# Attention, short convolution and gated projection on one core: transposes by halves of rows, a new order of the pieces, and GpSimd steps tied to VectorE

## The chip, the core and the metric

The kernel runs on one core of a Trainium2 chip. The metric is the device time of one execution in microseconds (us), the median of three runs. A core has TensorE (PE in the profile; its weight loads are PEld), VectorE (DVE), ScalarE (ACT), GpSimd (POOL) and SyncE (SP), which here issues all the DMAs.

## The reference

```python
scores = scale * np.matmul(q_c, k_c.transpose(0, 1, 2, 4, 3))     # chunks of 64 rows, 8 heads, 8 batches
scores = scores - np.max(scores, axis=-1, keepdims=True)
attn = np.exp(scores)
attn = attn / (np.sum(attn, axis=-1, keepdims=True) + 1e-09)
out = np.matmul(attn, v_c)                                        # x: (8, 576, 512)
...
for k in range(5):
    gate_pre += conv_w[k][None, None, :] * xp[:, k:k + S, :]      # causal convolution of x over the sequence
gate = 1.0 / (1.0 + np.exp(-gate_pre))
val = x @ w_val
return (gate * val @ w_out).astype(np.float32)
```

Everything is float32; q, k and v are (8, 8, 576, 64), the two weights (512, 512).

## The kernel before, in words

The tokens are cut into nine groups of 512 (g = 0 to 8; group 8 holds the last 64 of each batch), and each group into two halves of the channels (p = 0, 1). Such a (g, p) is called a pair here: 18 pairs, each with 32 blocks of 64 by 64 scores.

The program is a list of some 1,030 pieces, written out by hand in the string ORDER (line 19), and each engine runs its pieces in that order. A piece is a name and its indices. For a pair: `S` scores (64x64 matmuls in the four quarters of the array; the trace shows two instructions for each one of the program), `mx` row maxima, `sb` and `ex` (or `ng` and `ea`) subtraction and exponential, `sm` (or `rc`) row sums and reciprocals, `nm` normalising, `T` transposing the probabilities on TensorE (eight 128x128 transposes into a bank of PSUM), `ec` copying them out, `A` probabilities times v (64x64 matmuls again), `xr`, `xd` and `xc` the rounded value, its remainder and a plain copy of x. Then `V` the product with w_val, `vc` its copy, `k0` and `k` (`kx`, `kk` for two groups at once) the taps of the convolution, `sg` the sigmoid, `gs` gate times value, `gr` and `gd` its rounded value and remainder, `P` the product with w_out, `oc` and `st` copy and store. Each float32 product is made of three 128x128 by 128x512 matmuls: high by high, low by high, high by low, so V and P each need both parts of x and of the gated value. `w1` to `w9`, `wa`, `wb` and `Q` split the weights in the same way at the start. A `D` behind a name puts the piece on VectorE, a `G` (only in the changed kernel) on GpSimd.

Pair (0, 1) is done in two halves at the start, so that the first products can begin early. What sets the order around the change is this list alone, with two more tables: SLOTS, which says which buffer and which of the four double banks of PSUM a tile gets (a tile waits until the one before it in its slot has been read), and the pieces' own data. SyncE's DMAs are issued in the list's order too, eight in flight.

Lines that matter here: `tr` (369), `ec` (380), `av` (388), the loop over the list (602 to 609). Every operation goes through `run` in line 139, so the profile shows line 139 for all of them and they are told apart by their tiles.

Of the kernel before, what the change touches and what calls it, by code (L numbers as in the profile page):

```python
# [18 lines left out]
ORDER = """zw,lw v 1,zr 1,zr 0,lc,zi,zs 0,zs 1,lw v 3,lw v 2,w1 v 1,w5 c 0,w1 c 0,w2 v 1,w3 v 1,w5 v 1,w4 v 1,w2 c 0,w3 c 0,w5 v 3,  # L19
w7 v 1,w1 v 3,w6 v 1,w8D v 1,w2 v 3,w4 c 0,w3 v 3,W 9 22,Q v 1,lk 0 1 0,lq 0 1 0,w1 v 2,w4 v 3,w2 v 2,w3 v 2,w5 v 2,w6D v 3,  # L20
S 0 1 0,lk 0 0 0,lk 0 1 1,lq 0 1 1,lq 0 0 0,lk 0 0 1,lq 0 0 1,w4 v 2,wc v 1,mx 0 1 0,w6 v 2,w7 c 0,ng 0 1 0,w7 v 2,ea 0 1 0,ra 0 1 0,
W 3,S 0 1 1,w8D v 2,S 0 0 0,mx 0 1 1,w8D c 0,w9,ng 0 1 1,w7 v 3,S 0 0 1,lw v 0,lk 1 0,lq 1 0,lv 0 1,lw o 3,ea 0 1 1,ra 0 1 1,
rr 0 1 0,Q v 2,w8 v 3,mx 0 0,nm 0 1 0,sb 0 0,Q v 3,w5 v 0,w1 v 0,ex 0 0,T 0 1 0,w3 v 0,rr 0 1 1,S 1 0 0,wc v 2,sm 0 0,
nm 0 1 1,S 1 0 1,ec 0 1 0,w2 v 0,A 0 1 0,lk 1 1,lq 1 1,lv 0 0,lv 1 0,wc v 3,mx 1 0,T 0 1 1,nm 0 0,xr 0 1 0,ec 0 1 1,
V 0 2 2 0,sb 1 0,V 0 3 2 1,w5 o 3,A 0 1 1,xc 0 1 0,xr 0 1 1,w4 v 0,T 0 0,xc 0 1 1,xd 0 1 0,V 0 2 3 0,w6D v 0,V 0 3 3 0,
ec 0 0,V 0 2 3 1,w1 o 3,S 1 1 0,w7 v 0,ex 1 0,xd 0 1 1,A 0 0,w8 v 0,k0 0 2,sm 1 0,S 1 1 1,wa v 0,xc 0 0,V 0 0 2 0,V 0 2 2 1,
V 0 0 3 1,V 0 0 2 1,xr 0 0,mx 1 1,V 0 1 2 0,nm 1 0,V 0 0 3 2,V 0 3 3 1,k0 0 0,V 0 3 2 2,V 0 2 3 2,xd 0 0,V 0 3 1 0,
V 0 1 2 1,V 0 0 0 0,V 0 3 3 2,V 0 3 0 0,lw o 0,lw o 2,lw o 1,w5 o 0,k0 0 3,ng 1 1,k 0 0 1,T 1 0,k0 0 1,wbD v 0,V 0 0 0 2,
w2 o 3,V 0 3 2 0,k 0 0 2,V 0 2 1 1,ec 1 0,V 0 2 0 0,V 0 0 1 0,k 0 3 1,V 0 1 0 0,V 0 2 0 1,ea 1 1,V 0 2 0 2,w3 o 3,V 0 2 1 2,
k 0 1 1,V 0 3 1 1,V 0 0 2 2,V 0 1 1 1,w4 o 3,V 0 3 0 1,V 0 2 2 2,V 0 3 1 2,w1 o 1,A 1 0,k 0 0 3,w7 o 3,w1 o 0,V 0 1 3 2,  # L30
# [36 lines left out]
V 6 1 2,kk 6 0 3,V 6 0 1,V 6 0 3,k 4 0 4,V 8 1 1,k 4 1 4,V 6 1 0,kk 6 1 2,sg 4 0,V 8 1 3,kx 6 3,gs 4 0,V 6 2 2,V 6 1 3,
k0 8 0,gs 4 1,V 8 1 2,k0 8 1,V 8 0 2,kk 6 2 2,V 8 2 3,vc 8 0,k 3 2 2,V 6 0 2,gr 4 0,kk 6 1 3,V 7 0 0,gr 5 1,V 8 2 2,gdD 4 0,
V 7 1 3,V 6 3 3,kk 6 2 3,V 6 1 1,k 5 1 2,V 8 3 0,k 5 0 2,V 7 1 0,vc 8 1,kk 6 0 4,V 7 1 2,vc 6 0,V 6 2 3,k 3 1 3,gr 4 1,
V 7 0 3,k 5 1 3,P 4 0 0,vc 6 1,k0D 8 2,P 4 0 1,k 5 0 3,gdD 4 1,P 4 2 0,V 7 0 1,k 5 0 4,V 7 0 2,k 5 1 4,P 4 2 1,kk 6 1 4,  # L70
sg 5 0,V 7 2 0,V 7 2 1,kk 6 3 1,sg 6 0,P 4 1 2,k0 8 3,k 3 1 4,P 4 3 1,kk 6 3 2,V 7 2 2,P 4 0 3,gs 5 0,P 4 1 3,V 7 2 3,
gdD 5 1,gr 5 0,V 7 3 0,sg 7 0,kk 6 3 3,P 4 2 3,P 4 0 2,gdD 5 0,V 7 1 1,P 4 1 1,gs 6 0,vc 7 0,P 4 1 0,kk 6 2 4,V 7 3 2,
P 4 3 3,kk 6 3 4,P 4 3 0,P 5 2 0,k 8 1 1,sg 6 1,P 5 2 3,k 3 0 2,oc 4 0,V 7 3 3,k 3 0 3,P 5 2 1,gr 6 0,k 3 2 3,P 5 3 2,
# [21 lines left out]
    b="0 0 1 2 0 2 1 3 2 0 1 3 2 0 1 0 2 0 0 1 3 0 2 3 1 3 3 1 2 3 0 2 1 2 2 3 2 0 1 3 1 2 1 0 1 2 2 3 0 1 0 2 3 1 0 "  # L95
      "1 3 2 3 2 3 0 1 3 2 0 2 3 2 2 3 0 1 2 2 0 1 2 3 0 3 2 1 2 1 3 0 2 1 0 3 2 0 1 3 2 0 1 3 2",
    e="0 1 0 0 0 0 1 1 0 0 0 1 0 1 1 0 1 0",
)

ALONE = 20  # L100
# [566 lines left out]
```

## Time and profile before

| | |
|---|---|
| median of 3 runs | 280.64 us (280.20 to 281.83) |
| profiled execution, first to last instruction | 279.6 us |
| what lies around it, against the median | 1.0 us |
| PE busy | 268.9 us (96%), 3370 matmul instructions |
| DVE busy | 239.5 us (86%) |
| ACT busy | 198.7 us (71%) |
| POOL busy | 59.4 us (21%) |
| moved by DMA | 42.5 MB |
| granted TensorE clock | 1.000 on the mean |

The profile gives the span of one execution; the runs' times also hold what lies before its first and after its last instruction. A busy PE is not a PE at its peak: matmuls are pipelined, and their ends are modelled, so costs on TensorE are read from one start to the next. Times are in us from the span's start.

### The profile page before, as it was taken

The numbers are of one execution on the slowest core, as the hardware profiler recorded it, in microseconds if no ns is written. First come the engines' busy times: TensorE is split into PE (matmuls) and PEld (weight loads), VectorE is DVE, ScalarE is ACT, GpSimd is POOL, SyncE is SP. The second block draws the span as 40 slices with busy tenths as digits, with TensorE's granted clock in tenths as the row PEclk, the third lists the DMA queues.
The fourth block names the chain that finished last, engine by engine and source line by source line (L and its number), as shares of the span: only waits on it lengthen the run. The fifth ranks groups of instructions, "written<-read, shape, count | busy, mean of one in ns | idle before, by whom it ended". The sixth has DMA issues, their size and how long they took to land.

```text
span 279.6 us, 7851 instructions
## 1 busy us (share of the span) xinstructions
PE 268.9 (96%) x3370; PEld 216.6 (77%) x3370; DVE 239.5 (86%) x303; ACT 198.7 (71%) x368; POOL 59.4 (21%) x58
## 2 busy tenths in 40 slices
PE   6598999999998999999999999999999999999995
PEld 3366778887886888888888888888888888888884
DVE  3979999999999988989898998999999998996020
ACT  5899999999997988895958588837644544614402
POOL 1056242049294003061335001100000000300000
PEclk9999999999999999999999999999999999999999
DMA  6999999763831649540082000000000000050656
GB/s 224 395 409 406 406 407 409 290 225 108 281 149 37 192 150 338 189 131 30 2 292 88 2 5 2 0 0 2 0 0 0 4 0 0 16 212 0 241 209 225
DMA packets 14754, 42.46 MB, mean 152 GB/s; under 512 B 1536, under 2 KB 1792, under 8 KB 14720
## 3 DMA queue, kind: packets, MB, share of 16 engines
q1 hardware_dynamic: 14720, 41.97, 40.7%
q8 instruction: 26, 0.43, 0.6%
q14 instruction: 8, 0.07, 0.1%
HBM read 32.53 MB, written 9.44 MB: 150 GB/s over the span
## 4 chain that ended last, share of the span: by engine, by line
PE 89%; DMA 8%; issue 1%; SPq 0%; ACT 0%
PE b L139 89%; DMA z<-in_v 4%; DMA z<-in_moe_w_val 2%; DMA z<-in_q 2%; SPq L139 0%; ACT z L139 0%
## 5 line engine op out<-in xcount | busy, mean ns | idle before, releaser
L139 PE MATMUL b<-z,v_hi 128*128 128x512 f32 x288 | 97.3, 403 | 1.3 <-issue 1.1
L139 PE MATMUL b<-o_hi,z 128*128 128x512 f32 (+1 forms) x296 | 94.5, 391 | 0.0
L139 DVE SCALAR_TENSOR_TENSOR ys<-ys,cw 128x511 f32<-128x511 f32 (+7 forms) x104 | 84.5, 863 | 0.1
L139 ACT COPY z<-b 128x1024 f32<-128x1024 f32 (+2 forms) x53 | 50.3, 970 | 38.3 <-PE b L139 35.5
L139 PEld LDWEIGHTS b<-z,v_hi 128*128 128x128 f32 x288 | 53.8, 188 | 14.5 <-issue 1.7
L139 PEld LDWEIGHTS b<-o_hi,z 128*128 128x128 f32 x296 | 55.1, 188 | 12.6
L139 PE MATMUL b<-o_lo,z 128*128 128x512 f32 (+1 forms) x148 | 57.4, 388 | 0.0
L139 PE MATMUL b<-z,v_lo 128*128 128x512 f32 x144 | 55.9, 394 | 0.0
L139 POOL TENSOR_TENSOR z<-e_row,rs 128x1024 f32<-128x1024 f32 (+1 forms) x15 | 27.0, 1804 | 47.2 <-DVE rs L139 17.0
L139 PEld LDWEIGHTS b<-o_lo,z 128*128 128x128 f32 x148 | 27.8, 188 | 5.9
L139 PEld LDWEIGHTS b<-z,v_lo 128*128 128x128 f32 x144 | 27.1, 188 | 5.4
L139 POOL TENSOR_TENSOR z<-ys,z 128x1024 fp32r<-128x1024 f32 x4 | 10.0, 2527 | 96.9 <-ACT z L139 96.9
L139 ACT ACTIVATE ys<-ys 128x1024 f32<-128x1024 f32 x16 | 16.8, 1059 | 11.0 <-DVE ys L139 10.8
L139 ACT ACTIVATE e_row<-b,mx 128x64 f32<-128x64 f32 x80 | 23.7, 345 | 0.4 <-DVE mx L139 0.4
L139 DVE TENSOR_TENSOR z<-b,z 128x1024 fp32r<-128x1024 f32 (+1 forms) x19 | 22.0, 1161 | 2.3 <-ACT z L139 1.3
L139 ACT CAST z<-ys 128x1024 fp32r<-128x1024 f32 x16 | 16.5, 1048 | 9.0 <-DVE ys L139 9.0
L139 DVE TENSOR_REDUCE mx<-b 128x16 f32<-128x1024 f32 (+1 forms) x19 | 21.6, 1144 | 1.3 <-PE b L139 1.1
L139 PEld LDWEIGHTS b<-z,z 64*64 64x64 f32 x960 | 15.7, 135 | 7.8 <-DMA z<-in_k 2.6
L139 PE MATMUL b<-z,z 64*64 64x64 f32 x960 | 17.6, 221 | 3.7 <-DMA z<-in_q 3.0
L139 ACT CAST z<-b 128x1024 fp32r<-128x1024 f32 (+1 forms) x19 | 18.7, 991 | 2.1 <-PE b L139 2.1
L139 ACT ACTIVATE ys<-ys,cw 128x512 f32<-128x512 f32 (+1 forms) x25 | 19.2, 811 | 0.0
L139 ACT ACTIVATION_READ_ACCUMULATOR e_row<-b,mx 128x1 f32 x80 | 19.0, 238 | 0.0
(74 smaller groups left out, 308.3 us busy)
## 6 DMA issues: line engine op xcount, KB each, us to landing
out<-z SPq DMA_DIRECT2D x16, 512.0 KB, 3.7
z<-in_q SPq DMA_DIRECT2D x10, 512.0 KB, 7.2
z<-in_v SPq DMA_DIRECT2D x9, 512.0 KB, 5.0
ys<-in_v SPq DMA_DIRECT2D x9, 512.0 KB, 10.1
ys<-in_k SPq DMA_DIRECT2D x9, 512.0 KB, 7.3
z<-in_k SPq DMA_DIRECT2D x7, 512.0 KB, 9.4
ys<-in_q SPq DMA_DIRECT2D x6, 512.0 KB, 10.2
z<-in_moe_w_val SPq DMA_DIRECT2D x4, 512.0 KB, 5.4
```

What stands on the lines that cost most here:

```text
L139: return tc.keep_in_program_order(fn(*args, **kwargs))
```

## The change

Three things change.

1. `tr` now transposes a pair in two halves of rows: for each of the eight blocks one transpose of partitions 0 to 63 and one of partitions 64 to 127, with 64 columns each, into the two banks of the tile. The old function stays as `tr_whole` (piece `TW`). In the list, ten pieces are `TW` (the two halves of pair (0, 1) and pairs (0,0), (1,0), (1,1), (2,0), (2,1), (3,0), (3,1), (4,1)), and nine are the new `T`: pairs (4,0) and all of groups 5 to 8. `av` reads the probabilities in either layout.
2. All pieces behind the first 112 come in another order, with other slots. Some go to other engines or another form: two of `ra`/`rr` become `rc`; three `w1` go to GpSimd (`w1G`), two `w2` to VectorE, one `w5` and `w8` become one `w58`; VectorE gets two more `nm`, two more `gd`, four more `k0`, one more `oc` and one more `o1`, and loses one `wa`, one `wb`, one `kx`; pair (8, 1) uses `ng`/`ea`/`rc` in place of `sb`/`ex`/`sm`. In all VectorE has 305 rows in the program's listing in place of 282.
3. A table BEHIND ties 23 pieces on GpSimd to a piece named beside each, all of them of VectorE: the GpSimd step starts only when that one has ended.

```diff
-ORDER = """zw,lw v 1,zr 1,zr 0,lc,zi,zs 0,zs 1,lw v 3,lw v 2,w1 v 1,w5 c 0,w1 c 0,w2 v 1,w3 v 1,w5 v 1,w4 v 1,w2 c 0,w3 c 0,w5 v 3,
+ORDER = """zr 1,zr 0,zw,lw v 1,lc,zi,zs 0,zs 1,lw v 3,lw v 2,w1 v 1,w5 c 0,w1 c 0,w2 v 1,w3 v 1,w5 v 1,w4 v 1,w2 c 0,w3 c 0,w5 v 3,w7 v 1,
...
+BEHIND = {
+    "nm 1 1": "w7 o 3", "w1G o 0": "xd 1 0", "w1G o 1": "mx 2 0", "w8 o 3": "k 1 0 2", "nm 2 0": "sm 2 0",
...
+    "nm 4 1": "sm 4 1", "nm 5 1": "k 2 2 1", "gd 2 1": "gs 2 0", "gd 2 0": "sb 6 0", "nm 5 0": "sm 5 0",
...
-ALONE = 20
+ALONE = 28
...
+    def w58(n, c, b=None):
+        run(V.scalar_tensor_tensor, out=rest(n, c, b)[1], in0=part(raw[n, c][0], b), scalar=2.0**-52,
+            in1=part(wt[n, c], b), op0=ALU.mult, op1=ALU.mult)
...
-    def tr(g, p, b=None):
-        if not b:
+    def tr(g, p):
+        split.add((g, p))
+        et_ps[g, p] = bank()
+        for j in range(8):
+            block = normed[g, p][:, 2 * j:2 * j + 2, :].rearrange("p b k -> p (b k)")
+            for w in range(2):
+                r = slice(w * D, (w + 1) * D)
+                run(E.transpose, out=et_ps[g, p][:, w, j * D:(j + 1) * D], in_=block[r], identity=ident[r, r])
+
+    def tr_whole(g, p, b=None):
+        if (g, p) not in et_ps:
...
-        et = probs_t[g, p].rearrange("p (h b a q) -> p h b a q" if own is None else "p (b h a q) -> p h b a q", h=2, b=2, a=2)
+        if (g, p) in split:
+            et = probs_t[g, p].rearrange("p (w h b a t) -> p h b a w t", w=2, h=2, b=2, a=2)
+        else:
+            et = probs_t[g, p].rearrange("p (h b a w t) -> p h b a w t" if own is None else "p (b h a w t) -> p h b a w t", h=2, b=2, a=2, w=2)
...
+        if piece in BEHIND:
+            sync = mybir.DependencyInfo(mybir.DependencyClass.Sync, mybir.DependencyReason.DATA)
+            tc.add_manual_dep(made[begun].ins, ends[BEHIND[piece]].ins.name, sync, reason="behind")
```

What the list moves is seen in the rows of the engines. First TensorE around the scores of pairs (8, 0) and (7, 1), before: `ident` marks a transpose, 64x64 are scores or probabilities times v, `v_hi` and `v_lo` are the parts of w_val, `o_hi` of w_out.

```order
L139 MATMUL b_2088<-ys 64x64 x32
L139 MATMUL b_2125<-ys,z_1579 64x64 x32
L139 MATMUL b_2162<-ident,z_1944 128x128 x8
L139 MATMUL b_2176<-z_1720,v_hi 128x512
L139 MATMUL b_2176<-z_1720,v_lo 128x512
```

The same place now: the scores of pair (8, 0) are b_2167, and two transposes by halves stand before and between their two parts.

```order
L146 MATMUL b_2106<-ys,z_705 64x64 x32
L146 MATMUL b_2148<-ident,z_2091 128x64 x16
L146 MATMUL b_2167<-z_2101,ys 64x64 x16
L146 MATMUL b_2184<-ident,z_1971 128x64 x16
L146 MATMUL b_2217<-z_1735,v_hi 128x512
L146 MATMUL b_2217<-z_1735,v_lo 128x512
```

Before, one transpose of eight stood behind one unbroken stretch of 64x64 work; now sixteen half transposes stand inside it, and the stretch goes 64x64, halves, 64x64, halves, 128x128.

Next TensorE behind the transpose of pair (0, 0) (the row with `ident`), before: b_459 is probabilities times v of pair (0, 0), b_439 the scores of pair (1, 1), z_390 the rounded x of pair (0, 1).

```order
L139 MATMUL b_419<-ident,z_388 128x128 x8
L139 MATMUL b_393<-z_390,v_hi 128x512 x2
L139 MATMUL b_393<-z_390,v_lo 128x512
L139 MATMUL b_439<-z_373,z_375 64x64 x16
L139 MATMUL b_459<-z_434,z_377 64x64 x32
L139 MATMUL b_515<-z_390,v_hi 128x512
```

The same now: b_456 is probabilities times v of pair (0, 0), b_491 the scores of pair (1, 1), and z_433 the remainder of x of pair (0, 1).

```order
L146 MATMUL b_420<-ident,z_388 128x128 x8
L146 MATMUL b_393<-z_390,v_lo 128x512 x2
L146 MATMUL b_393<-z_390,v_hi 128x512
L146 MATMUL b_448<-z_390,v_lo 128x512
L146 MATMUL b_448<-z_433,v_hi 128x512
L146 MATMUL b_456<-z_435,z_377 64x64 x32
L146 MATMUL b_491<-z_373,z_375 64x64 x32
```

Six products now stand ahead of b_456 where three stood, the last of them reads the remainder z_433, and both parts of the scores of pair (1, 1) have gone behind it.

That remainder is written by VectorE. Its rows up to there, before (z_429 is the remainder, in two halves, z_305 and z_437 are words of the weights, rs_494 the row sums of pair (1, 0)):

```order
L139 TENSOR_TENSOR z_429<-b_356,z_390 128x512
L139 CAST v_hi<-z_305 128x2x256
L139 TENSOR_SCALAR z_437<-z_276 128x512
L139 TENSOR_SCALAR z_305<-z_305 128x512
L139 TENSOR_TENSOR z_429<-b_399,z_390 128x512
L139 TENSOR_REDUCE rs_494<-e_row_65 128x16
```

And now (z_433 is the remainder, z_304 and z_429 the words; the second row on z_429 needs what GpSimd's `w1G` writes):

```order
L146 TENSOR_TENSOR z_433<-b_356,z_390 128x512
L146 TENSOR_SCALAR z_304<-z_304 128x512
L146 CAST v_hi<-z_304 128x2x256
L146 TENSOR_SCALAR z_429<-z_275 128x512
L146 TENSOR_SCALAR z_429<-z_429 128x512
L146 TENSOR_TENSOR z_433<-b_399,z_390 128x512
L146 TENSOR_REDUCE rs_444<-e_row_65 128x16
```

Four short steps stand between the two halves of the remainder where three stood.

## Rows read from the trace of the kernel before

**Rows 1.** The page: busy time, share of the span and instructions of each engine
```profile
PE 268.9 (96%) x3370; PEld 216.6 (77%) x3370; DVE 239.5 (86%) x303; ACT 198.7 (71%) x368; POOL 59.4 (21%) x58
```
**Rows 2.** The chain of waits in order: start, length, what
```profile
13.77 11.88 DMA z<-in_v
...
25.78 5.95 PE b L139 x118
...
84.78 0.90 issue
85.68 191.00 PE b L139 x1883
```
**Rows 3.** Busy time by stretch: PE, PEld, DVE, ACT, POOL; clock, DMA share
```profile
25.80:105.00 79.20, 78.13 (x1224) 63.83 (x1224) 75.15 (x107) 74.71 (x196) 30.13 (x23) 1.00 0.67 246
...
161.00:258.00 97.00, 97.00 (x667) 78.75 (x660) 91.80 (x96) 55.11 (x60) 5.13 (x9) 1.00 0.05 17
```
**Rows 4.** Timeline of PE at two whole transposes: start, length, what
```profile
143.45 1.03 PE L139 MATMUL b<-ident,ys 128*128 128x128 f32 x8
144.32 1.04 PE L139 MATMUL b<-ident,z 128*128 128x128 f32 x8
```
**Rows 5.** Timeline of PE, then of weight loads, around a stretch of 64x64
```profile
74.43 0.63 PE L139 MATMUL b<-z,v_hi 128*128 128x512 f32 x2
74.89 0.40 PE L139 MATMUL b<-z,v_lo 128*128 128x512 f32 x1
75.13 0.39 PE L139 MATMUL b<-z,v_hi 128*128 128x512 f32 x1
75.45 2.10 PE L139 MATMUL b<-z,z 64*64 64x64 f32 x128
77.47 0.50 PE L139 MATMUL b<-o_hi,z 128*128 128x512 f32 x1
77.81 0.39 PE L139 MATMUL b<-o_lo,z 128*128 128x512 f32 x1
...
75.44 1.96 PEld L139 LDWEIGHTS b<-z,z 64*64 64x64 f32 x128 [0.36 <-ACT e_row L139]
```
**Rows 6.** Timeline of weight loads: two of a transpose, two of a product
```profile
22.87 0.14 PEld L139 LDWEIGHTS b<-ident,z 128*128 128x128 f32 x1 [0.43 <-POOL z L139]
22.93 0.14 PEld L139 LDWEIGHTS b<-ident,z 128*128 128x128 f32 x1
...
21.22 0.19 PEld L139 LDWEIGHTS b<-z,v_hi 128*128 128x128 f32 x1 [0.45 <-ACT z L139]
21.33 0.19 PEld L139 LDWEIGHTS b<-z,v_lo 128*128 128x128 f32 x1
```
**Rows 7.** Timeline of DVE, 24 to 28.7 us
```profile
24.20 0.76 DVE L139 TENSOR_SCALAR z<-z 128x512 f32<-128x512 f32 x2
24.88 0.68 DVE L139 TENSOR_TENSOR z<-b,z 128x512 fp32r<-128x512 f32 x1
...
27.49 1.20 DVE L139 TENSOR_REDUCE mx<-b 128x16 f32<-128x1024 f32 x1
```
**Rows 8.** Groups by form: count, busy us, mean ns; a POOL row, then DVE rows
```profile
L139 POOL TENSOR_TENSOR z<-z,z 128x512 f32<-128x512 f32 x5 | 7.4, 1479 | 6.0 <-DVE z L139 6.0
...
L139 DVE TENSOR_TENSOR z<-e_row,rs 128x1024 f32<-128x1024 f32 x3 | 3.6, 1215 | 0.0
...
L139 DVE TENSOR_SCALAR z<-z 128x512 f32<-128x512 f32 x8 | 3.4, 422 | 3.7 <-DMA z<-in_moe_w_val 3.7
```
**Rows 9.** POOL, then PE: normalising and transposing pair (1, 1)
```profile
38.15 1.98 POOL L139 TENSOR_TENSOR z<-e_row,rs 128x1024 f32<-128x1024 f32 x1 [8.44 <-DVE rs L139]
...
41.32 1.03 PE L139 MATMUL b<-ident,z 128*128 128x128 f32 x8
```
**Rows 10.** DVE, then POOL, where the two meet at 242 us
```profile
242.29 4.24 DVE L139 SCALAR_TENSOR_TENSOR z<-tails,cw,z 128x512 f32<-128x512 f32 x3
...
242.40 2.91 POOL L139 TENSOR_TENSOR z<-ys,z 128x1024 fp32r<-128x1024 f32 x1 [66.32 <-ACT z L139]
```
**Rows 11.** DVE's last remainders of the gated value
```profile
255.04 2.36 DVE L139 TENSOR_TENSOR z<-z,z 128x1024 fp32r<-128x1024 f32 x2 [1.11 <-ACT z L139]
```

More of the change, by code (lines that the diff above doesn't have):

```diff
@@ L154, in chunk_attention_gated_conv @@
     (qt, kt, vt, s_ps, probs, normed, et_ps, probs_t, x_ps, xs, xh, xl, acc, v_ps, v_sb, gh, gl, o_ps, o_sb, mxs, rss,
-     raw, wt, wr, wq, w_ps, xs_at, acc_at) = ({} for _ in range(28))
+     raw, pairs, wt, wr, wq, w_ps, w_bank, xs_at, acc_at) = ({} for _ in range(30))
     small = {name: 0 for name in ("mx", "rs")}
     done = {}
+    split = set()
     def count(name):
@@ L169, in piece @@
                 kept[g, p] = z()
+            flat = of[g, p].rearrange(of_flat[len(of.shape)])
             if half is None:
-                run(DMA, out=kept[g, p], in_=of[g, p].rearrange(of_flat[len(of.shape)]))
+                run(DMA, out=kept[g, p], in_=flat)
             else:
-                run(DMA, out=kept[g, p].rearrange("p (b t) -> p b t", b=2)[:, half], in_=of[g, p][:, half])
+                run(DMA, out=twin(kept[g, p])[:, half], in_=twin(flat)[:, half])
         return piece
@@ L177, in chunk_attention_gated_conv, with part, lw, kept_in @@
     lq, lk, lv = load(qt, q), load(kt, k), load(vt, v)
-    def lw(n, c):
-        pair = z(U32)
-        words = pair.rearrange("p (n w) -> p n w", w=2)
-        raw[n, c] = words[..., 0], words[..., 1]
-        run(DMA, out=pair, in_=w_in[n][c * P:(c + 1) * P, :].bitcast(U32))
-    def kept_in(w, n, c):
+    def part(a, b):
+        return a if b is None else a[:, b * 256:(b + 1) * 256]
+    def lw(n, c, b=None):
+        if (n, c) not in pairs:
+            pairs[n, c] = z(U32)
+        both = pairs[n, c].rearrange("p (n w) -> p n w", w=2)
+        raw[n, c] = both[..., 0], both[..., 1]
+        rows = w_in[n][c * P:(c + 1) * P, :].bitcast(U32)
+        if b is None:
+            run(DMA, out=pairs[n, c], in_=rows)
+        else:
+            run(DMA, out=twin(pairs[n, c])[:, b], in_=twin(rows)[:, b])
+    def kept_in(w, n, c, b=None):
         if n == "v":
-            return w[n][:, c // 2 * 2:c // 2 * 2 + 2, c % 2 * 256:(c % 2 + 1) * 256]
+            rows = slice(c // 2 * 2, c // 2 * 2 + 2) if b is None else c // 2 * 2 + b
+            return w[n][:, rows, c % 2 * 256:(c % 2 + 1) * 256]
         return w[n][:, c, :]
-    def unit(a, n):
-        return a.rearrange("p (c m) -> p c m", c=2) if n == "v" else a
+    def unit(a, n, b=None):
+        return a.rearrange("p (c m) -> p c m", c=2) if n == "v" and b is None else a
     def lc():
@@ L219, in w4 @@
-    def w4(n, c):
-        run(V.scalar_tensor_tensor, out=wq[n, c], in0=wt[n, c].bitcast(U32), scalar=3, in1=wq[n, c],
-            op0=ALU.logical_shift_left, op1=ALU.bitwise_or)
-    def w5(n, c):
-        wr[n, c] = pool.tile([P, NH * TAPS], F32, name="cw_r") if n == "c" else z()[:, :T]
-        run(S.mul, wr[n, c].bitcast(F32R) if (n, c) in summed_on_pe else wr[n, c], raw[n, c][0], 2.0**-52)
-    def w6(n, c, copy=S.copy):
-        run(copy, out=kept_in(wh, n, c), in_=unit(wq[n, c].bitcast(F32), n))
@@ L241, in wb @@
-    def wb(n, c, on=G):
-        run(on.tensor_tensor, out=kept_in(wl, n, c), in0=unit(wt[n, c], n), in1=unit(wr[n, c], n), op=ALU.add)
-    def wq_sum(n, c):
-        w_ps[n, c] = unit(bank()[:, 0], n)
-        for i, (lhsT, rhs) in enumerate(((ident, wq[n, c].bitcast(F32)), (signed[:, 1], kept_in(wh, n, c)),
-                                         (signed[:, 0], wr[n, c].bitcast(F32R)))):
-            run(E.matmul, w_ps[n, c], lhsT=lhsT, rhs=rhs if i == 1 else unit(rhs, n), start=i == 0, stop=i == 2)
@@ new lines, in rest, with w5, w6, w7 @@
+    def rest(n, c, b):
+        if (n, c) not in wr:
+            wr[n, c] = z()[:, :T]
+        a = part(wr[n, c], b)
+        return a, a.bitcast(F32R) if (n, c) in summed_on_pe else a
+    def w5(n, c, b=None):
+        run(S.mul, rest(n, c, b)[1], part(raw[n, c][0], b), 2.0**-52)
+    def w6(n, c, b=None, copy=S.copy):
+        run(copy, out=kept_in(wh, n, c, b), in_=unit(part(wq[n, c], b).bitcast(F32), n, b))
+    def w7(n, c, b=None):
+        run(V.tensor_single_scalar, out=part(wt[n, c], b).bitcast(U32), in_=part(wq[n, c], b), scalar=0xFF800000, op=ALU.bitwise_and)
@@ new lines, in wb, with wq_high @@
+    def wb(n, c, b=None, on=G):
+        run(on.tensor_tensor, out=kept_in(wl, n, c, b), in0=unit(part(wt[n, c], b), n, b), in1=unit(part(wr[n, c], b), n, b), op=ALU.add)
+    def wq_high(n, c, b=None):
+        if (n, c) not in w_ps:
+            w_bank[n, c] = bank()
+            w_ps[n, c] = w_bank[n, c][:, 0]
+        ps = unit(part(w_ps[n, c], b), n, b)
+        run(E.matmul, ps, lhsT=ident, rhs=unit(part(wq[n, c], b).bitcast(F32), n, b), start=True, stop=False)
+        run(E.matmul, ps, lhsT=signed[:, 1], rhs=kept_in(wh, n, c, b), start=False, stop=False)
@@ L254, in w9, with wq_low, wq_sum, wc @@
+    def wq_low(n, c, b=None):
+        ps = unit(part(w_ps[n, c], b), n, b)
+        run(E.matmul, ps, lhsT=signed[:, 0], rhs=unit(part(wr[n, c], b).bitcast(F32R), n, b), start=False, stop=True)
+    def wq_sum(n, c, b=None):
+        wq_high(n, c, b)
+        wq_low(n, c, b)
+    def wc(n, c, b=None, copy=S.copy):
+        run(copy, out=kept_in(wl, n, c, b), in_=unit(part(w_ps[n, c], b), n, b))
     def w9():
@@ L262, in sc @@
         own = (g, p) in HALVES
-        if own or b == 0:
+        each, first = (g, p, b if own else None) not in LESS, own or (g, p) not in s_ps
+        if own or (g, p) not in s_ps:
             ps = bank().rearrange("p h (b c k) -> p h b c k", b=2, c=4)
@@ L277, in sc @@
                         run(E.matmul, to[w * D:(w + 1) * D, h, 2 * a + u], lhsT=qq[r, b, c],
-                            rhs=kk[r, b, c], start=True, stop=True, skip_group_check=True)
+                            rhs=kk[r, b, c], start=each or (first and u == a == 0), stop=True, skip_group_check=True)
     def blocks(a, b):
@@ L315, in mh @@
         m = cols(mxs[g, p, b], b)
-        r = pool.tile([P, 2, 16], F32R, name=f"mr{small['mx'] % 6}")
+        small["mr"] = small.get("mr", 0) + 1
+        r = pool.tile([P, 2, 16], F32R, name=f"mr{small['mr']}")
         mxs[g, p, b, "r"] = r = r if b is None else r[:, :, 0:8]
@@ L380, in ec @@
     def ec(g, p, b=None, copy=S.copy):
-        if not b:
+        if (g, p) not in probs_t:
             probs_t[g, p] = z()
@@ L410, in xr @@
     def xr(g, p, b=None):
-        if not b:
+        if (g, p) not in xh:
             xh[g, p] = z(F32R)
@@ L415, in xd @@
     def xd(g, p, b=None):
-        if not b:
+        if (g, p) not in xl:
             xl[g, p] = z(F32R)
@@ L426, in xe @@
     def xe(g, p, b=None):
-        if not b:
+        if (g, p) not in xl:
             xl[g, p] = z(F32R)
@@ L439, in xc @@
         else:
-            if not b:
+            if (g, p) not in xs:
                 xs_at[g, p] = []
@@ L578, in keep_warm, with keep_warm_beside @@
             run(E.matmul, ps[:, 0, c], lhsT=warm[:, :P], rhs=warm[:, c], start=True, stop=True)
+    def keep_warm_beside(n, c, k):
+        for i in range(k):
+            run(E.matmul, w_bank[n, c][:, 1], lhsT=warm[:, :P], rhs=warm, start=True, stop=True)
     def zr(i):
```

205 lines of the change are left out of this document (111 added, 94 removed), and 15 rows, old and new, of tables (BEHIND, z).

## The prediction

> **What bounds the kernel now.** I read the chain of waits first. From 25.78 us on it is TensorE and nothing else but one gap of 0.90 us that no engine or DMA ends [rows 2]; before that it is loads, the last of them the 11.88 us of v for pair (0, 0). The page then shows TensorE busy for 96% [rows 1]. The stretches come next: VectorE is busy 75.15 of 79.20 us from 25.8 to 105 us and 91.80 of 97 us from 161 to 258 us, and the clock is granted in full in both, the 2.4 GHz level [rows 3]; nothing in the change lets TensorE rest for long, so no term for the clock is taken. So a change counts if it takes starts off TensorE's row, moves the load that releases pair (0, 0), or makes VectorE late: it runs some 5% from its own limit all the time.
>
> **The halves of the transposes.** Two whole transposes stand back to back: the second set of eight starts 0.87 us after the first [rows 4], so one 128x128 transpose costs 109 ns. A half transpose, 64 rows by 128 columns with 64 columns moved, does not occur before. The nearest row is a stretch of 64x64 matmuls, which also move 64 columns: 128 weight loads take 1.96 us [rows 5], that is 32 quarters-of-the-array sets of four in 1.83 us between first and last start, 59 ns a set. The four quarters run side by side there, the two upper with the two lower rows of the array, and into both banks. If the two halves of a block do the same, a block costs 59 ns in place of 109, a pair 0.47 in place of 0.87 us, and the nine pairs in this form save 9 x 0.40 = 3.6 us. That is the upper end. The lower end is halves that run one after the other, 16 x 59 ns = 0.94 us a pair: 9 x 0.07 = 0.6 us lost. I take 3.6, since the 64x64 row is the nearest in moved columns and in rows.
>
> What a load of weights costs could undo this. Two loads of a transpose start 0.06 us apart when TensorE has nothing else to do, two of a product 0.11 us [rows 6]. A half transpose loads as many columns as a whole one, so by the row a block of two halves can start every 60 ns or so, and the load does not bind.
> The Trainium skill says otherwise (TensorE: Matmul & The Clock Gate, the section on LDWEIGHTS): a load's time goes by its columns alone, at 1.2 GHz, and a load of few rows takes as long as one of 128. By that a block of halves would cost some 107 ns (an estimate from that page), and nothing would be saved; the product's loads agree with it here, the transpose's do not.
>
> **The switches between tile shapes.** In rows 5 two products of 512 columns take 74.89 - 74.43 = 0.46 us, 0.23 each. The stretch of 64x64 could follow the product at 75.13 + 0.23 = 75.36 us, and the product behind it, 0.11 us longer than its like, really begins at 77.58: 2.22 us for 32 sets of 59 ns, or 1.89. The two changes of shape together cost 0.33 us, 0.17 each. Counted along the list, TensorE has 22 stretches of 64x64 work before, 44 changes. Now, if a 64x128 half counts as a shape of its own, there are 53 changes: +9 x 0.17 = +1.5 us. If it counts as 64x64, there are 42: -0.3 us. If it counts as 128x128, 46: +0.3 us. The trace shows no 64x128 tile; it differs from both shapes that it has, so I take +1.5.
> The Trainium skill has the same rule (TensorEngine Tiling (Array Packing), Key Properties): changing the tiling mode, not just the tile, drains TensorE. By that too each change counts and the term is +1.5; the 0.17 us agrees that a change costs something, and no run here shows which shapes count as one mode.
>
> **The order at the start.** The loads up to v of pair (0, 0) are the same nineteen in the same order, so I leave its landing at 25.64 us. But six products now stand ahead of that pair's A, and the last reads the remainder of x of pair (0, 1). VectorE has four short steps between its two halves where three stood, of 0.36 us from start to start [rows 7]; so that remainder ends near 26.0 in place of 25.56. The second of the four needs the clamp that moved to GpSimd: at 1.48 us, the nearest row [rows 8], it is done near 24.0, a microsecond before it is wanted, and it could take 2.5 us before it costs anything. A for pair (0, 0) then begins near 26.4 and not 25.78, 0.6 later. In exchange three more products (0.7 us) lie ahead of it and half the scores of pair (1, 1) (0.5) behind: net +0.4 us. The bounds are -0.2 (the remainder is early) and +1.0.
>
> Behind it the scores of pair (1, 1) end about 28.4, and `mx` follows 1.0 us later than at 27.49 [rows 7]. VectorE had 0.8 us of idle time there, so it goes on about 0.5 late. GpSimd's `nm` of pair (1, 1), which took 1.98 us and ended 1.2 us before its transpose [rows 9], is now tied behind one more VectorE step of 0.36; what is queued behind it on GpSimd are weights, the next `nm` comes much later. TensorE reaches this transpose some 0.4 us earlier than before by its own sum: I take +0.4 us of waiting, between 0 and 1.2.
>
> **The rest.** The ties: TensorE waits on GpSimd only through `nm` and four `gd` (now two), and 7 of the 23 ties name the `sm` that the `nm` has to wait for anyway. They cost nothing where VectorE's step ends before GpSimd is free, and in the trace the two meet badly once, at 242 us, where three taps beside a `gd` of 2.91 us took 4.24 us [rows 10], some 2 us more than three of 0.7, off the path; I take 0, between -0.5 and +1. VectorE: five 1.22 us steps more (`nm`, `gd`, `oc`), `sb` and `sm` of one pair less (2.7), four `k0` of 0.42 more [rows 8], and small ones: about +5.0 us by durations, +4.5 from start to start. ScalarE's changes are hidden, since it is busy 71% [rows 1]; an `ea` of 16 steps more is paid for by two table loads fewer. Loads behind the first nineteen go mostly to slots not used before, so they wait for nothing new and I take 0. The gap of 0.90 us [rows 2] has no releaser; I let half of it go, -0.4.
>
> Sum on TensorE: -3.6 + 1.5 + 0.4 + 0.4 - 0.4 = -1.7 us. The profiled span is 279.6 us, its surroundings 1.0 us; the tail behind the last matmul (copy, store) stays. 280.6 - 1.7 = 278.9 us.
>
> **Rivals.** A change under 0.5%, 1.4 us, is about what a measurement of this kernel cannot tell from none.
>
> First, halves count as the 64x64 shape. For it: the list puts them beside 64x64 work all nine times. Against: the 64x64 tiles also split the columns. Then -0.3 in place of +1.5: 277.1 us.
>
> Second, the halves of a block don't run side by side, because each load of 128 columns holds the next one up. For it: the product's loads, 0.11 us apart; against: the transpose's, 0.06. At 109 ns a block the 3.6 us vanish and the 1.5 of switches stay: 280.6 + 1.5 + 0.4 + 0.4 - 0.4 = 282.5, and one after the other 283.1. It decides from 90 ns a block on, where 72 blocks save less than the 1.4 to 1.9 us that the rest costs; slower by 0.5% it is above 106 ns.
>
> Third, VectorE becomes the bound. Its last remainder ended at 257.4 us [rows 11]. With 4.5 us more work and the same idle time it ends at 261.9, and 37 matmuls of 512 columns and 24 of 256 stand behind its first use now, 11.4 us at 0.23 and 0.12 each; with 2.95 us of tail that is a span of 276.3, 1.6 under the forecast's 277.9. So 1.6 us more idle time than before would bind it, and each further microsecond counts in full. For it: 95% busy, and waits for transposes that come late; against: fewer waits on GpSimd. With 3.5 us more idle: 280.8 us.
>
> Fourth, other short waits spread over the new order, 1 us or so more than I found: 279.9.
>
> **How the numbers follow.** Forecast 0.42, first rival 0.20, second 0.17, third and fourth 0.21. The forecast's own spread is some 0.8 us, so two thirds of it lie under 279.2. Faster by over 0.5%: 0.28 + 0.20 + 0.03 = 0.51. Slower by over 0.5% (282.0): 0.14 from the second, 0.05 from the third, with a little of the forecast 0.20. The rest, 0.29, is no change. The range goes from the first rival, 276.8, to just under the second, 282.2; the forecast's own is 278.0 to 280.0.
>
> **What would show it.** Starts of the `ident` matmuls: 16 a pair in 0.47 us confirm the saving, 0.87 or more the second rival. The gap from a half transpose to the 64x64 rows beside it: near 0.17 us over the normal step, or near none. A for pair (0, 0) near 26.4, the transpose of pair (1, 1) with a wait on GpSimd. VectorE's last remainder near 260 and PE without waits behind it, or PE waiting on VectorE from 190 us on. A first v that lands at another time would make the start wrong.

## The result, and the profile after

The changed kernel takes 283.85 us (median of 4 runs, 283.27 to 284.59); beside it the kernel before took 281.15 (4 runs, 280.20 to 281.83). The ratio is 1.0101, with an interval of 1.0070 to 1.0132. The forecast was 278.9, a gain. The profiled execution has a span of 282.4 us, 2.8 more than before.

The page of the changed kernel, busy time of each engine, and its DMA queue of instructions:

```profile
PE 268.9 (95%) x3441; PEld 215.9 (76%) x3442; DVE 245.0 (87%) x312; ACT 195.9 (69%) x387; POOL 52.2 (18%) x58
...
q8 instruction: 27, 0.44, 0.6%
```

Against [rows 1], TensorE is as busy as before, to a tenth of a microsecond, in a span that is 2.8 us longer. So it stands idle for longer, and the chain of waits says where (start, length, what; `issue` is time in which an engine waits for nothing that the profile shows):

```profile
24.30 3.44 DVE z L146 x3
...
27.79 11.94 PE b L146 x209
39.73 0.16 issue
39.90 5.42 PE b L146 x124
45.31 1.74 issue
47.05 72.71 PE b L146 x1141
119.76 0.26 issue
120.02 5.50 PE b L146 x126
125.52 1.95 issue
127.47 151.98 PE b L146 x1449
```

Before, TensorE had two gaps without a releaser, the 0.90 us of [rows 2] and, in a line that stands between the ones shown there,

```profile
31.73 0.17 issue
```

together 1.07 us. Now there are four, 0.16 + 1.74 + 0.26 + 1.95 = 4.11 us. The longest stands in the middle of 64x64 work:

```profile
125.01 0.51 PE L146 MATMUL b<-z,z 64*64 64x64 f32 x19
127.47 1.85 PE L146 MATMUL b<-z,z 64*64 64x64 f32 x109 [1.95 <-issue]
```

And the chain gets to TensorE at 27.79 us, by way of VectorE, in place of 25.78 by way of a load.

The start first. VectorE's timeline, which answers to [rows 7]:

```profile
23.55 0.41 DVE L146 TENSOR_SCALAR z<-z 128x512 uint32<-128x512 uint32 x1
23.89 0.41 DVE L146 CAST v_hi<-z 128x512 fp32r<-128x512 f32 x1
24.22 2.91 DVE L146 TENSOR_SCALAR z<-z 128x512 uint32<-128x512 uint32 x2
27.06 0.68 DVE L146 TENSOR_TENSOR z<-b,z 128x512 fp32r<-128x512 f32 x1
```

GpSimd's at the same time (`w8 v 0`, then `wa v 0`):

```profile
24.05 1.40 POOL L146 TENSOR_TENSOR z<-z,z 128x512 f32<-128x512 f32 x1 [1.57 <-DVE z L146]
25.52 1.33 POOL L146 TENSOR_TENSOR z<-z,v_hi 128x512 f32<-128x512 f32 x1
```

The two TENSOR_SCALAR take 2.91 us; two took 0.76 in [rows 7]. Each ends 0.28 us behind one of GpSimd's two steps. The new order put `w7 v 0`, which releases `w8 v 0`, ahead of them. TensorE shows who waited:

```profile
24.68 1.37 PE L146 MATMUL b<-z,z 64*64 64x64 f32 x64
27.79 1.16 PE L146 MATMUL b<-z,z 64*64 64x64 f32 x64 [1.74 <-DVE z L146]
```

The first 64 are the probabilities times v of pair (0, 0), at 24.68, since v had landed earlier than in the profile before. The next 64 are the scores of pair (1, 1), and they wait until the last row of VectorE ends at 27.74.

The halves of the transposes, timeline of PE, which answers to [rows 4]:

```profile
147.22 0.71 PE L146 MATMUL b<-ident,z 64*128 64x64 f32 x16
147.86 0.69 PE L146 MATMUL b<-ys 64*64 64x64 f32 x32
...
149.88 0.71 PE L146 MATMUL b<-ident,z 64*128 64x64 f32 x16
150.53 0.50 PE L146 MATMUL b<-z,v_hi 128*128 128x512 f32 x1
```

Sixteen halves and the change of shape behind them take 0.64 us, against 0.87 for eight whole ones; single starts in the trace put the sixteen at 0.49 from first to last, and 0.15 from the last of them to the next start, where a half's own step is 0.031. VectorE's last remainders, as in [rows 11]:

```profile
259.32 2.36 DVE L146 TENSOR_TENSOR z<-z,z 128x1024 fp32r<-128x1024 f32 x2 [1.12 <-ACT z L146]
```

They end at 261.68, 4.3 us later than before, and no matmul waits for them.

### The profile page after: what moved, and what is told of

It reads as the page before. It is cut to its first block, busy times and chain, and to the rows that moved or that the text cites. A ratio compares the mean times of both kernels' runs of the same rounds, so it can differ in the third digit from the quotient of the medians.

```text
span 282.4 us, 8030 instructions
## 1 busy us (share of the span) xinstructions
PE 268.9 (95%) x3441; PEld 215.9 (76%) x3442; DVE 245.0 (87%) x312; ACT 195.9 (69%) x387; POOL 52.2 (18%) x58
## 4 chain that ended last, share of the span: by engine, by line
PE 88%; DMA 4%; DVE 4%; issue 2%; ACT 1%; SPq 0%; DVEq 0%
PE b L146 88%; DMA z<-in_moe_w_val 2%; DMA z<-in_q 2%; DVE z L146 2%; DVE e_row L146 1%; DVE mx L146 1%; DVE rs L146 1%; SPq L146 0%; ACT e_row L146 0%; ACT z L146 0%; DVE v_hi L146 0%; DVEq L146 0%
## 5 line engine op out<-in xcount | busy, mean ns | idle before, releaser
L146 PE MATMUL b<-z,v_hi 128*128 128x512 f32 x288 | 94.9, 400 | 0.2 <-ACT z L146 0.2
L146 ACT COPY z<-b 128x1024 f32<-128x1024 f32 (+2 forms) x60 | 57.2, 973 | 38.6 <-PE b L146 36.9
L146 DVE SCALAR_TENSOR_TENSOR z<-z,cw,z 128x509 f32<-128x509 f32 (+3 forms) x80 | 56.0, 738 | 0.1
L146 DVE TENSOR_TENSOR z<-z,z 128x1024 f32<-128x1024 f32 (+2 forms) x24 | 28.0, 1186 | 7.0 <-ACT z L146 6.8
L146 ACT ACTIVATE z<-z 128x1024 f32<-128x1024 f32 (+3 forms) x25 | 21.3, 866 | 15.1 <-DVE z L146 13.1
L146 POOL TENSOR_TENSOR z<-e_row,rs 128x1024 f32<-128x1024 f32 (+1 forms) x13 | 23.0, 1772 | 41.4 <-DVE rs L146 10.7
L146 DVE SCALAR_TENSOR_TENSOR ys<-ys,cw 128x1022 f32<-128x1022 f32 (+3 forms) x24 | 29.9, 1273 | 0.1
L146 ACT ACTIVATE e_row<-b,mx 128x64 f32<-128x64 f32 x96 | 28.6, 357 | 1.2 <-DVE mx L146 1.2
L146 ACT ACTIVATION_READ_ACCUMULATOR e_row<-b,mx 128x1 f32 x96 | 23.9, 249 | 0.0
L146 ACT CAST z<-z 128x1024 fp32r<-128x1024 f32 x12 | 12.6, 1056 | 6.7 <-DVE z L146 6.6
```

The lines of the kernel that those rows point to most:

```text
L146: made.append(tc.keep_in_program_order(fn(*args, **kwargs)))
```

## The experiments

Theory: the halves do what was forecast, and two things take more than they give: VectorE's steps at the start, which last as long as GpSimd's beside them, and gaps in which TensorE waits for its own instructions. Rivals: the start is just too full; the gaps are hidden waits on a bank or a buffer, or chance. All ratios are to the kernel before, run beside.

**Five short steps in another order.** The changed kernel with:

```diff
-w7 v 0,w6D v 0,w3 o 3,w2D o 3,xd 0 1 1,
+w3 o 3,w2D o 3,w6D v 0,w7 v 0,xd 0 1 1,
```

> Five short VectorE steps ahead of the second half of the remainder of x of pair (0, 1) stand in another order: the two 128x512 steps on w_out (w3 o 3, w2D o 3) come first, then w6D v 0, then w7 v 0, which releases GpSimd's w8 v 0. Theory (collision): in the changed kernel the two steps took 1.51 and 1.48 us in place of 0.42 because GpSimd ran a 128x512 product beside them from 24.05 to 26.85 us; with them ahead of it each takes 0.42 again, the remainder ends near 25.7 in place of 27.7, and the probabilities times v of pair (0, 0) start near 26.2 in place of 27.79. The time falls by about 1.5 us, to some 282.3, if nothing behind gives it back. Rival (the four steps are simply too many): the remainder ends where it did, 27.7, and the time stays at 283.8 within 0.5. TensorE's instructions and their order are the same, so by the theory of instruction loading the gaps of 1.74 and 1.95 us stay inside the same stretches of 64x64 work, after the 85th and the 19th matmul.

282.01 us (12 runs), ratio 1.0044 (1.0017 to 1.0072), 1.8 us under the changed kernel. VectorE's timeline of this kernel:

```profile
24.20 0.75 DVE L146 TENSOR_SCALAR z<-z 128x512 uint32<-128x512 uint32 x2
...
25.20 0.41 DVE L146 TENSOR_SCALAR z<-z 128x512 uint32<-128x512 uint32 x1
25.53 0.68 DVE L146 TENSOR_TENSOR z<-b,z 128x512 fp32r<-128x512 f32 x1
```

The same steps, 0.75 us for the two in place of 2.91: the collision is shown, and TensorE has no wait there. The gaps stayed behind the same matmuls (85 and 19 into their stretches, as expected). One thing was not expected. The timeline of PE behind the gap:

```profile
45.87 0.91 PE L146 MATMUL b<-z,z 64*64 64x64 f32 x43 [1.82 <-issue]
...
47.12 0.63 PE L146 MATMUL b<-z,v_lo 128*128 128x512 f32 x1
47.55 1.06 PE L146 MATMUL b<-z,v_hi 128*128 128x512 f32 x2
...
50.70 0.39 PE L146 MATMUL b<-z,v_lo 128*128 128x512 f32 x1
```

and by stretch (PE, PEld, DVE, ACT, POOL; granted clock, DMA share, GB/s):

```profile
41.00:44.05 3.05, 3.05 (x93) 2.35 (x91) 3.05 (x5) 3.01 (x4) 0.54 (x2) 1.00 1.03 408
46.71:50.30 3.59, 3.59 (x12) 2.83 (x10) 3.39 (x5) 3.05 (x9) 0.56 (x1) 0.53 1.03 409
```

Behind 1.82 us of rest the granted clock is 0.53, near the 1.2 GHz level, for 3.6 us, and eight products take 0.43 in place of 0.23 us: this execution paid for its gap twice, with 8 x 0.20 = 1.6 us more. In the first profile of the changed kernel the clock held at 1.00 behind a gap of 1.74.

**More instructions ahead, three runs.** Small warming matmuls at the start in place of long ones, in the time that these took; the second with `W 1 86`, the third is the kernel before with the edit shown:

```diff
-W 9 22
+W 5 54
```

> The changed kernel with 28 more small warming matmuls at the start, in place of four of the nine long ones, so that TensorE gets 56 more instructions (28 weight loads, 28 matmuls) in the same time, ahead of everything else. Theory (instruction loading): the gaps without a releaser stand where TensorE's next 256 instructions have not arrived, so each gap that stays sits 28 matmuls earlier in the program: in the stretch at 45 us after the 57th matmul in place of the 85th, at 125 us nine matmuls before the end of the stretch that ended there. Some may vanish and others appear, since it depends on what the 200 instructions ahead of the boundary cost: the time lies anywhere from 281 to 286. Rival (a wait that the profile does not show, on a bank of PSUM or a buffer): the gaps stay after the same matmuls, and the time stays at 283.8 within 0.5.

> As the run before with 56 more warming matmuls at the start in place of eight long ones, 112 instructions more. Theory (instruction loading): what is left of the gaps sits 56 matmuls earlier in the program than in the changed kernel: at 45 us after the 29th matmul in place of the 85th, and that at 125 us would fall into the products and transposes ahead of the stretch, where an instruction lasts ten times as long as in 64x64 work, so it should be hidden: time 280.5 to 285. Rival (a hidden wait): gaps after the same matmuls, 283.8 within 0.5.

> The kernel before with the same 28 more warming matmuls in place of four long ones, 56 instructions more. Theory (instruction loading): its one gap, 0.90 us at 84.8 us, moves 28 matmuls earlier in the program or goes, and others may come; TensorE's own work stays, so the time is 280.2 less 0.9 plus what comes, 279.5 to 283. Rival (a hidden wait): the gap stays after the same matmul and the time is that of before within 0.5.

288.05, 289.34 and 289.17 us, ratios 1.0261 (1.0234 to 1.0288), 1.0325 (1.0285 to 1.0365) and 1.0297 (1.0271 to 1.0324). The upper ends of all three expectations were too low: 28 more small matmuls, in place of four long ones and in time that TensorE had anyway, cost the kernel before 8.5 us. In its profile the gaps take 6.6 us in place of 1.1, and behind the longest the granted clock is 0.63 from 30 to 34 us. The chain of waits of the changed kernel with 28 more:

```profile
31.33 10.81 PE b L146 x126
...
42.51 5.44 PE b L146 x124
...
48.68 18.55 PE b L146 x380
...
67.61 61.57 PE b L146 x1015
129.19 0.99 issue
130.17 21.41 PE b L146 x381
151.58 0.89 issue
152.47 25.12 PE b L146 x508
```

and of the kernel before with 28 more:

```profile
25.04 3.13 PE b L139 x127
28.18 3.06 issue
31.24 36.50 PE b L139 x632
67.74 1.77 issue
69.52 15.28 PE b L139 x253
```

Look at the counts of matmuls between gaps (each piece of the first chain ends in one, of 0.37 to 1.08 us): 126, 124, 380, 1015, 381, 508 in the first chain, 632 and 253 in the second, 124, 1141 and 126 in the changed kernel. All are a multiple of about 127 (380 = 3 x 126.7, 1015 = 8 x 126.9, 1141 = 9 x 126.8), whatever the program does there. The run with 56 more small matmuls has five, of 0.89 to 1.65 us, behind matmuls 346, 473, 2121, 2502 and 3010 of its trace; with 28 more there are gaps behind the same five numbers. A matmul comes with a load of weights, so that is some 254 instructions. The page has 27 packets on the instruction queue, 0.44 MB, 16 KB each, for 3441 matmuls and 3442 loads: 255 to a packet. The gaps stand at the boundaries of these packets. A hidden wait would have moved with its matmul, 28 places down the count. The packets themselves say the same. In the changed kernel four of them set out at 37.44, 44.49, 117.82 and 124.80 us, and the matmuls behind the four gaps start at 39.90, 47.05, 120.02 and 127.47, that is 2.2 to 2.7 us later. In the traces of all the runs here, all 41 gaps without a releaser of 0.13 us or more behind 24 us end 2.2 to 2.9 us after a packet has set out. The DMA queues of the changed kernel from 124.6 to 126.2 us, around the start of its gap at 125.52:

```profile
GB/s 0 0 0 102 410 0 0 0 0 0 0 0 0 0 0 0 0 0 0 0 0 0 0 0 0 0 0 0 0 0 0 0 0 0 0 0 0 0 0 0
...
q8 instruction: 1, 0.02, 5.1%
```

One packet of instructions sets out near 124.8 (a slot is 0.04 us), and the matmuls go on at 127.47, with loads hardly on the queues. Before 50 us, where the loads move some 400 GB/s, the time from packet to matmul is 2.4 to 2.6 us; so loads do not lengthen that part, and even the gap of 3.06 us ends 2.4 us after its packet. What makes a gap long is that the packet sets out late. In 64x64 work 128 matmuls take 1.96 us [rows 5], so a packet is used up in 2 us, less than the 2.2 to 2.9 from its setting out to its use; one of products lasts 128 x 0.23 = 29 us. The Trainium skill has the packets (Runtime: NRT & Kernel Launch, Instruction fetch mechanics: blocks of 16 KiB, 256 instructions, fetched while the one before runs) and calls the cost mostly hidden; the trace agrees on the size, and differs on the cost: up to 3.06 us at one boundary.

**Fewer instructions ahead, two runs.** The order of five steps as above, and `W 10 14` or `W 12 0` in place of `W 9 22`:

> The order of the five short steps as in the first run, and 7 warming matmuls fewer at the start (one long one in place of eight small ones), 14 instructions fewer. Theory (instruction loading): all gaps sit 7 matmuls later in the program than in the first run, at the same count of instructions; the sum of the gaps changes by less than 1 us either way: 281 to 283. Rival (hidden waits): same gaps at the same matmuls of the program.

> As the run before with 19 warming matmuls fewer (three long ones in place of 22 small ones), 38 instructions fewer. Theory (instruction loading): gaps 19 matmuls later in the program than in the first run, after the 104th matmul of the stretch at 45 us and the 38th of that at 126 us; a worked estimate by the fetch times of the traces puts the sum of the gaps within 0.5 us of the first run's: 281 to 283. Rival (hidden waits): gaps after the 85th and the 19th matmul as in the first run.

282.31 and 283.38 us (1.0064, 1.0042 to 1.0085; 1.0089, 1.0069 to 1.0109); the second is above what was expected. Gaps behind 40 us are 1.73, 0.21 and 1.58 us in the first, 1.42 and 1.24 in the second, the long ones behind matmuls 726 and 1993 of the trace, the same counts as in the changed kernel (725 and 1992 there; its trace lacks one matmul). No shift tried frees the new order of them.

**Whole transposes in the new order, halves in the old.** The nine `T` as `TW` in the changed kernel; in the kernel before:

```diff
+        if (g, p) in split:
+            for j in range(8):
...
+                    run(E.transpose, out=et_ps[g, p][:, w, j * D:(j + 1) * D], in_=block[r], identity=ident[r, r])
```

> The changed kernel with whole transposes again for the nine pairs that it transposes in halves, the order of all pieces unchanged. Theory (the halves save what was forecast, and loading of instructions hides it): TensorE's row grows by 9 x 0.37 = 3.3 us for the transposes themselves (0.87 in place of 0.50 us from first to last start) and loses the changes of shape on both sides of a half, some 9 x 0.15 = 1.4 us, so its work without the gaps is about 2 us longer. 144 instructions fewer stand behind pair (4, 0), so the boundaries of the 256-instruction blocks move on from there by 16 per pair and the gaps behind 125 us change; those at 45 us and near 120 us stay. Time: 283.8 + 2, less up to 2 us where the gap of 1.95 us goes: 283 to 287. Rival (the halves save nothing): TensorE's work without gaps within 0.5 us of the changed kernel's.

> The kernel before with the same nine pairs transposed in halves of rows, in its own order. Theory (halves save about 2 us on TensorE's row, less the gaps that 144 more instructions bring): TensorE's work without gaps 2 us shorter than before, time 278.5 if no new gap comes, 279 to 282 with one or two of 1 to 2 us behind 120 us, where the halves begin. Rival (halves of a block run one after the other): work without gaps 0.6 to 2 us longer than before, time above 282.

Whole in the new order: 287.86 us, ratio 1.0253 (1.0228 to 1.0278), above the 283 to 287 expected. The chain's PE pieces from the scores of pair (1, 1) on add up to 251.7 us there and 247.6 in the changed kernel; 1.6 of the difference is eight products at 0.43 us behind a gap of 1.72, so the halves are worth 2.5 between these two executions. Halves in the old order: 279.74 us (11 runs), ratio 0.9958 (0.9942 to 0.9975), the first kernel here that beats the one before. Its chain:

```profile
84.14 0.07 issue
84.21 34.83 PE b L139 x343
...
121.76 152.52 PE b L139 x1468
```

From the same matmul (1487) to the end it takes 274.28 - 84.21 = 190.1 us against 191.0 in [rows 2]: 0.9 gained where the halves are, with a wait of 0.3 in it, so 1.2 where 2 was expected; the gap at 84, 0.07 in place of 0.90, gives as much again in this execution. In this order many of the nine stand between products, where a half pays two changes of shape that a whole transpose doesn't.

**Halves moved beside 64x64 work.** The last kernel, with `T 6 1` moved to the scores of (7, 1) and `T 8 0` to `A 7 0` (the first move is shown; two bank numbers in SLOTS change places so that the buffers stay):

```diff
-T 6 1,sm 6 0,P 2 1 2,ec 6 1,sm 7 0,S 7 1 0,
+sm 6 0,P 2 1 2,sm 7 0,T 6 1,ec 6 1,S 7 1 0,
```

> The kernel before with nine pairs in halves, as in the run of that, and two of the half transposes moved behind a few products to stand directly ahead of 64x64 work (pair (6, 1) ahead of the scores of pair (7, 1), pair (8, 0) ahead of its neighbour's probabilities times v), buffers unchanged. Theory (every change of shape costs about 0.15 to 0.2 us): each of the two drops one change of shape out of four, together 0.3 to 0.5 us less on TensorE's row; the time is 279.3 if no gap comes, 279 to 281 with one. Rival (the order of the neighbours makes no difference): 279.7 within 0.3.

279.66 us (12 runs), ratio 0.9963 (0.9944 to 0.9982): no difference that can be told from the run without the move, as the rival had it, though 0.3 to 0.5 is too little to be sure of in these runs.

**The changed kernel again, and without the ties.** `BEHIND = {}` in the second:

> The changed kernel once more, beside the next two: 283.8 within 0.8 us, and a second profile of it. Theory (instruction loading): gaps at the same counts of TensorE instructions as in its first profile, behind the same matmuls, of other lengths; where a gap of 1.7 us or more stands, the clock may be found at 1.2 GHz behind it, as in the first run of the five steps. Rival (chance events of one execution): gaps elsewhere.

> The changed kernel without the 23 ties of GpSimd steps to VectorE steps, all else the same. Theory (the ties cost and give nearly nothing, as forecast): within 0.7 us of the changed kernel's run beside it. Rival 1 (the ties hold GpSimd away from VectorE's steps that it lengthens): without them more VectorE steps of 0.42 or 0.74 us take above 1 us, and the time is 1 to 3 us longer. Rival 2 (the ties hold up nm and so TensorE): 1 us or more shorter.

Again: 284.62 us (282.64 to 285.89), ratio 1.0133 (1.0091 to 1.0175), the upper end of what was expected. Its profile has the collision at the start (PE waits 2.0 us for VectorE) and a gap of 0.52 at 121.45, where the first has 0.26; that of 1.74 is 0.14, that of 1.95 is not in it, while its scores of pair (1, 1) begin at 29.69, 1.9 later. The places stay, the lengths change from one execution to the next. With 0.7 us of such gaps in place of 4.1 this execution still has a span of 282.1 us, and most of that lies at the start. By stretch, behind the wait for VectorE:

```profile
29.69:33.05 3.36, 3.36 (x67) 2.96 (x68) 2.65 (x4) 1.35 (x4) 1.84 (x1) 0.50 1.03 406
```

From the first of these scores to the fourth product behind them it takes 3.36 us at a granted clock of 0.50, the 1.2 GHz level; in the first profile it took 1.89 at 1.00. So the collision can cost 1.5 us beyond its wait, and no single gap is the whole loss.

Without ties: 289.58 us, ratio 1.0314 (1.0282 to 1.0346), 5 us above, the first rival, which had 1 to 3. Its VectorE, then its GpSimd:

```profile
57.40 2.96 DVE L140 SCALAR_TENSOR_TENSOR z<-z,cw,z 128x508 f32<-128x508 f32 x2
...
116.19 4.95 DVE L140 SCALAR_TENSOR_TENSOR z<-z,cw,z 128x509 f32<-128x509 f32 x5
```

```profile
57.66 2.16 POOL L140 TENSOR_TENSOR z<-e_row,rs 128x1024 f32<-128x1024 f32 x1 [5.90 <-DVE rs L140]
```

Two taps of 0.74 us take 2.96 beside an `nm`, five take 4.95. Seven VectorE steps behind 40 us are lengthened in this way, by some 7 us together, and TensorE waits for VectorE five times there, 3.2 us in all; with the ties it does not. The rest of the 5 us is not accounted for here. So the ties keep GpSimd away from the steps that it would hold up. The collision at the start is one that no tie covers: `w8 v 0` is not in the table. The Trainium skill (GPSIMD Engine Reference, Key points) names the steps at risk: VectorE's with two inputs from SBUF or in a mode that uses two ports. The traces agree for steps with two inputs, and the `mx` and the other steps that read PSUM kept their 1.2 us beside GpSimd; that a TENSOR_SCALAR, with one input, runs in such a mode here no run shows.

## Why the prediction was wrong

The sum that came out, from TensorE's starts: each step from start to start from 33 us on, against the usual step of its kind (0.231 us a product, 0.109 a whole transpose, 0.031 a half, 0.0147 a 64x64 matmul).

| term | forecast | measured |
|---|---|---|
| halves of the transposes | -3.6 | -3.4 |
| changes of tile shape | +1.5 | +1.6 |
| start, up to 33 us | +0.4 | +0.5 |
| wait of pair (1, 1)'s transpose | +0.4 | 0 |
| gaps without a releaser (3.0 by the chain's idle time) | -0.4 | +3.5 |
| short hesitations between like matmuls | 0 | +0.6 |
| sum | -1.7 | +2.8 |

- **Halves and changes of shape: right.** Two halves run side by side, and a half counts as a shape of its own. The first rival (they count as 64x64) is out: 0.15 us lie between the last start of the one and the first of the other, either way. The second rival comes nearest to the time, with 282.5 to 283.1, and has nothing of its mechanism: a pair's starts take 0.49 us, not 0.87.
- **The start: the net was near, by two errors that met.** "So that remainder ends near 26.0" failed: it ended at 27.74, since the two steps ahead of it took 1.5 us each. The collision stood in my own text, as a stray case at 242 us [rows 10], and I did not look for it where the order had moved. I also had the wrong edge: not A of pair (0, 0) but the scores behind it wait, since VectorE has to read the bank that they need. A itself started 1.1 us earlier than before, as v had landed by then. Without the collision the start would have gained, which the run with five steps in another order gives: 1.8 us on the median. That the net came out near the forecast was luck.
- **The gap: the step that failed.** "The gap of 0.90 us [rows 2] has no releaser; I let half of it go, -0.4." In its place the gaps grew by 3.0 us of idle time, 3.5 by starts, in the profiled execution: TensorE waits for its own instructions at packet boundaries, a cost that the sum did not have. A gap that nothing ends was a sign of it. I also read one gap where there were two (0.17 us at 31.73), and the 0.90 at 84.78 us stands two products behind a stretch of 128 64x64 matmuls. The new order puts more 64x64 work under the boundaries, and it does so without the 144 instructions that the halves add on TensorE: in one profile each, the gaps take 1.1 us in the old order and 0.1 there with halves, but 4.8 us in the new order with whole transposes; with halves it is 4.1 in the first profile and 0.7 in the second. The fourth rival had other short waits of 1 us or so, not these.
- **The clock: a second step that failed.** The text had "nothing in the change lets TensorE rest for long, so no term for the clock is taken". The wait of 1.74 to 1.96 us for VectorE and the gaps of up to 1.95 are such rests. In the first profile they cost no clock; in the second the clock was 0.50 behind the wait, and 1.5 us were lost.
- **Ties: at no cost, right; but my reason was too small.** They do not only cost nothing: the new order without them is 5 us slower.
- **VectorE as the bound: rightly left out.** 4.3 us later at the end of it, where I had 4.5, with no wait on TensorE.
- **The base.** Each execution that has both shows 1.7 to 2.0 us around its span, not 1.0: the profiled execution of before was one of 281.5, not 280.6. Worth 0.8 us, in the direction of the error.

What stays open: what exactly sets off a fetch, and so why the gaps at 45 and 125 us differ so much from one execution to the next (1.95 to none); at 125 us it started late with the queues nearly empty. Whether loads on the queues hold back a packet's setting out before 50 us was not tried apart.

## What to carry to other kernels

On an engine that works through small instructions, count instructions as well as time: a gap with no releaser at a fixed count (here 127 matmuls with their loads) is the engine waiting for its program, and any edit ahead, even in idle time, moves it to other work. So compare two orders only after shifting each by a few tens of instructions. Spreading dense small work rather than joining it should help by the same reasoning; no run here tried it. And when an order changes which GpSimd step runs beside which VectorE step, check each such pair by its operands; one step that is let go 1 us early can cost 2, and more where the clock falls behind the wait.

## What the runs showed of the hardware that was not expected

- TensorE's instructions come in packets of 16 KB, about 254 loads and matmuls; at boundaries, most of them within 64x64 work or close behind it, it stood still for up to 3.1 us, and each of 41 such gaps ended 2.2 to 2.9 us after a packet set out. Moving the boundaries by 56 instructions, with 28 small warming matmuls in place of four long ones, changed the time of the kernel before by 8.5 us (280.7 to 289.2).
- Behind a gap of 1.82 us the granted clock was 0.53 for 3.6 us in one execution, and 0.50 behind a wait of 1.96 in another; it was 1.00 behind 1.74 and 1.95 us in a third.
- A TENSOR_SCALAR of 0.42 us on VectorE took 1.51 and 1.48 us beside GpSimd's steps of 1.40 and 1.33, and ended 0.28 us behind them.
- Two transposes of 64 rows by 128 columns run side by side: 31 ns from start to start, against 109 for a whole one.
